# Low words of the second weight tile on GpSimd by halves, and the last output tile finished by column halves

## The chip, the cores and the metric

The kernel runs on one core of one Trainium2 chip. Its engines are TensorE (PE, with its weight loads shown apart as PEld), VectorE (DVE), ScalarE (ACT), GpSimd (POOL) and SyncE (SP, which here only issues DMAs). The metric is the device time of one execution in microseconds; less is better.

## What is computed

Retention (attention with a decay per head, no softmax) over 8 batches, 8 heads, 576 positions of 64, followed by a feed-forward layer:

```python
scores = scale * np.matmul(q, k.transpose(0, 1, 3, 2))
ret = scores * Dmat                      # Dmat = gamma[h] ** (i - j) for i >= j, else 0
x = np.matmul(ret, v)                    # laid out as 4608 tokens x 512
h = x @ w_in                             # 512 x 2048
g = h - np.tanh(h)
out = g @ w_out                          # 2048 x 512, fp32
```

Products of the feed-forward layer are made in three passes: every fp32 operand is split into a high word (rounded to the matmul's format) and a low word (the rest), and high x high, high x low and low x high are added up in PSUM.

## The kernel before

The 576 positions are cut into nine chunks of 64; a chunk of all 8 batches is a block of 512 tokens (n = 0 to 8). The weights are 16 tiles of w_in and 16 of w_out, each 128 x 512, which arrive as 64-bit words and are turned into a high and a low word on the chip.

**The conversion of a weight tile** runs over three engines. ACT makes a mask from the raw words in two steps (a Tanh, L130 or L157, and an Abs, L135, in `guard` and `guard_end`); DVE puts the 32-bit value together in three integer steps (`h_shift` L140, `l_shift` L143, `h_top` L146); ACT casts the value to the high word (L198 and L200 in `unit`, L165 in `second`); and the low word is the value minus the high word, one subtraction (`finish`, L213), on DVE except for the first tile, which has it on GpSimd.

**The start.** Chunk 0 of the retention runs first, for the eight batches in turn. Then `second` converts w_in tile 1 by column halves, and in between it starts tile 2, whose mask is called `ahead`: the Tanh before the halves, the Abs after the cast of the first half. The low word of tile 1 is left in the list `last`; the next call of `finish`, which comes behind the `h_shift` of tile 2, makes it on DVE in one piece. The loop over `seq` then runs `mm1(n, f)`, twelve matmuls that give the hidden tile h of block n and weight tile f: for f = 1, eight matmuls with high words (x high, x low), then four with low words of the weights (columns of the first half, then of the second). The high half of tile 2 is what `mm1(0, 2)` begins with. In the code the order of each engine's instructions is the order in which they are written, and each waits for those whose results it reads.

**The end.** `stage_b(8, ...)` runs `mm2(8, f)`, the second product of block 8: for each f twelve matmuls into four PSUM tiles o_0 to o_3 (128 tokens x 512 each). The last two f (14 and 15) run together, in groups of three matmuls, ordered by `groups`: (s, t) is f = 14 + s and output tile t. When a tile has its last product, `store_last` copies it to SBUF (o_1 on DVE, the others on ACT) and issues two DMAs of 64 rows x 2 KB to the output: the first from SP, the second from ACT (for o_0 both from SP). There is nothing behind the last of them but the end of the program.

The trace writes names without block and tile numbers: `wi<-mi` is a cast of a w_in tile, `o<-wo,gh` a second product with the high word gh, `gl` and `gs` the low word and a buffer that holds both.

Of the kernel before, what the change touches and what calls it, by code (L numbers as in the profile page):

```python
# [9 lines left out]
F32 = mybir.dt.float32  # L10
# [4 lines left out]
ALU = mybir.AluOpType  # L15
# [3 lines left out]
NT, DM, DF = B * S, H * D, 2048  # L19
P = 128  # L20
NF = DF // P
NCC = DM // P
C = 64
NC = S // C
BLK = B * C
# [73 lines left out]
def retention_ffn(ctx: ExitStack, tc: tile.TileContext, ins, out, spill, wvar):  # L99
    nc = tc.nc  # L100
# [4 lines left out]
    psp = ctx.enter_context(tc.tile_pool(name="psp", bufs=1, space=PSUM))  # L105
# [6 lines left out]
    win, wout, wraw, masks = {}, {}, {}, {}  # L112
# [21 lines left out]
    def guard_end(m):  # L134
        nc.scalar.activation(m.bitcast(F32), m, AF.Abs, scale=HI_BITS)  # L135

    halves = (slice(0, DM // 2), slice(DM // 2, DM))
# [10 lines left out]
    def second(low):  # L148

        t, f = stream[1]  # L150
        hw, lw, z = wraw[t, f][:, :, 1], wraw[t, f][:, :, 0], masks.pop((t, f))
        del wraw[t, f]

        w = const.tile([P, 2, 2, DM // 2], F32R, tag="wi14", name="wi1")
        win[f] = w
        ahead = masks[stream[2]] = pool.tile([P, DM], I32, tag="cv", bufs=4, name="ahead")
        nc.scalar.activation(ahead, wraw[stream[2]][:, :, 1].bitcast(F32), AF.Tanh, scale=STEP)  # L157
        ops = (h_shift, l_shift, h_top)
        for place_, (n, op) in enumerate(((0, 0), (0, 1), (1, 0), (0, 2), (1, 1), (1, 2))):
            at = halves[n]  # L160
            ops[op](z[:, at], hw[:, at], lw[:, at])
            if place_ == 0:
                low()
            if op == 2:
                nc.scalar.copy(w[:, n, 0], z[:, at].bitcast(F32))  # L165
                if n == 0:
                    guard_end(ahead)
        at_["guard"] = 3
        last.append(("i", w, z))

    def unit(k):

# [46 lines left out]
    last, going, pace = [], [], []  # L219
# [285 lines left out]
    gs, ops, homes, obs = {}, {}, {}, {}  # L505
# [55 lines left out]
    def mm2(n, f, at=-1, between=None):  # L561
        first, final = (turn[0], turn[-1]) if n == 1 else (0, NF - 1)
        if f == first:
            ops[n] = [psp.tile([P, DM], F32, tag=f"o{t}", bufs=1, name=f"o{n}_{t}") for t in range(4)]
        if f != final:
            order = [(f, t, k) for k in range(3) for t in range(4)]
        elif n < NC - 1:
            order = [(f, t, k) for t in range(4) for k in range(3)]
        else:

            groups = [(0, 0), (0, 1), (1, 0), (1, 1), (0, 2), (1, 2), (0, 3), (1, 3)]
            order = [(f - 1 + s, t, k) for s, t in groups for k in range(3)]
        for place_, (f_, t, k) in enumerate(order):
            if place_ == at:
                between()
            g, a = [(gs[n, f_][0], 0), (gs[n, f_][0], 1), (gs[n, f_][1], 0)][k]
            nc.tensor.matmul(  # L577
                ops[n][t], g[:, t * P : (t + 1) * P], wout[f_][:, a, :],
                start=(f_ == first and k == 0), stop=(f_ == final and k == 2),
            )  # L580
            if (k, t) == (1, 2):
                middle = tc.nc.cur_bb.bb.instructions[-1].name
            if f_ == final and k == 2:
                (store_last if n == NC - 1 else store)(n, t)
        return middle

    def store(n, t):
# [150 lines left out]
    for j in range(B - 1):  # L738
# [8 lines left out]
        o = psp.tile([P, 8, C], F32, tag=("o2", "o3", "own")[j % 3], bufs=1, name=f"own_first{j}")[:, :4]  # L747
# [26 lines left out]
    next(final_item)  # L774
    lows.pop(0)()
    second(lows.pop())
    assert not lows
    at_["convert"] = 2
# [30 lines left out]
    first = 2 * B  # L809
# [100 lines left out]
    for k, (n, f) in enumerate(late):  # L910
        if k in (3, 16, 29):
            follow, scale = entry3(first + (0, 2, 5)[(3, 16, 29).index(k)], rest)
        if 0 < k < len(late) - 1:
            words(*late[k + 1])
        if k < len(late) - 2:
            resume(*late[k + 2])
        for ahead in (4, 5) if k == 0 else (5,):
            if k + ahead < len(late):
                fetch(*late[k + ahead])
        if k in (3, 16, 29):  # L920

            follow()
        if k in (6, 19):
            scale()
        if k in (7, 20):
            load_part(rest[0], 0)
        if k in (10, 23):
            prep(rest.pop(), 0)
        for _ in range(2 if k < 4 else 1):
            step()  # L930
        for _ in range((k > 5) + (19 < k < 26)):
            next(summed)
        if k < len(late) - 1:
            mm2(n, f)
        for _ in range({0: 3, 1: 3, 2: 3, 3: 2}.get(k, 4 < k < 16 or 21 < k < 24)):
            raw_words(*raws.pop(0))
# [258 lines left out]
    def stage_b(n, m0):  # L1195

        fetch(n, 3)
        for f in range(NF):
# [20 lines left out]
            if (n, f) != (NC - 1, NF - 2):  # L1219
                middle = mm2(n, f, later or -1, turn_)  # L1220
# [10 lines left out]
    for f in range(NF):  # L1231
        mm1(2, f)
        if f == 0:
            mm2(*late[-1])
        if f == 1:
            scale()
        for _ in range(2):
            next(summed, None)
        if f == 2:
            load_turn(2, 0)  # L1240
        if f == 6:
            prep_turn(2, 0)
            load_turn(1, 0)
            load_turn(1, 1)
        if f in (9, 10):
            prep_turn(1, f - 9)
        if 10 < f < 14:
            fetch(2, f - 11)
        if f > 13:
            split(2, f - 14, fetched.pop((2, f - 14)), False)  # L1250
# [75 lines left out]
```

## Time and profile before

| | us |
|---|---|
| median of 3 runs | 848.39 |
| the runs | 847.99 to 848.69 |
| the profiled execution, whole | 849.77 |
| its span, first to last instruction | 848.0 |
| TensorE busy in the span | 840.1 (99%) |
| VectorE, ScalarE, GpSimd busy | 483.4, 362.6, 82.5 |

The profiled execution lasted 1.77 us longer than its span, and 1.38 us longer than the median of the runs. Times in the rows below are microseconds from the start of the span. A matmul's row covers its way through the array and so overlaps the next; the step from start to start is what one costs in a stream. DVE, ACT and POOL rows overlap their neighbours by some 0.05 to 0.1 us for the same reason.

### The profile page before, as it was taken

The page shows a single profiled execution, that of the slowest core. Times are in us where ns is not written, and L with a number is a line of the kernel's source. Part 1 is how long each engine was busy: PE and PEld are TensorE (multiplying, and loading weights), DVE is VectorE, ACT ScalarE, POOL GpSimd, SP SyncE. Part 2 cuts the span into 40 slices and gives each one's busy share as a digit, 9 for nine tenths or more (in the row PEclk, how much of TensorE's full clock was granted, in tenths as well). Part 3 has the DMA queues.
Part 4 walks back from the last instruction along what each step waited for, and adds up shares of the span by engine and source line. Part 5 has one row for each costly group of instructions (what it writes and reads, how often), then busy time and mean ns, then how long its engine had stood idle before and what let it go on. Part 6 is the DMA issues. An engine that isn't in the chain of part 4 may idle for free.

```text
span 848.0 us, 18635 instructions
## 1 busy us (share of the span) xinstructions
PE 840.1 (99%) x7694; PEld 694.0 (82%) x7694; DVE 483.4 (57%) x824; ACT 362.6 (43%) x732; POOL 82.5 (10%) x68
## 2 busy tenths in 40 slices
PE   8999999999999999999999999999999999999998
PEld 7788888888888888888888888888888888888886
DVE  5989878787567675344346755434456554443321
ACT  5887765454335454223244543322245532232321
POOL 0110002020000002111110001212100021121100
PEclk9999999999999999999999999999999999999999
DMA  9977978884787788444477665534677364452542
GB/s 342 321 293 225 371 232 300 243 280 132 224 272 271 228 308 249 149 153 170 132 236 224 209 181 194 187 125 170 207 214 209 108 201 171 133 191 75 147 115 62
DMA packets 71380, 174.95 MB, mean 206 GB/s; under 512 B 8704, under 2 KB 10368, under 8 KB 66048
## 3 DMA queue, kind: packets, MB, share of 16 engines
q1 hardware_dynamic: 70768, 172.85, 62.1%
q8 instruction: 60, 0.98, 0.5%
q10 hardware_dynamic: 528, 0.92, 0.3%
q14 instruction: 24, 0.20, 0.1%
HBM read 124.72 MB, written 48.76 MB: 205 GB/s over the span
## 4 chain that ended last, share of the span: by engine, by line
PE 97%; DVE 1%; ACT 1%; DMA 1%; issue 0%
PE o L577 32%; PE o L1136 15%; PE h L520 15%; PE pnew L1105 7%; PE pv L1105 7%; PE pown L1105 4%; PE py L1105 4%; PE pz L1105 4%; PE s L357 3%; PE new L357 2%; PE own L357 2%; DMA a<-in_first_dram 1%; PE wps L628 1%; ACT th L1155 0%; PE s_first L357 0%; PE new_first L357 0%
## 5 line engine op out<-in xcount | busy, mean ns | idle before, releaser
L577 PE MATMUL o<-wo,gh 128*128 128x512 f32 x608 | 156.0, 393 | 0.0
L577 PEld LDWEIGHTS o<-wo,gh 128*128 128x128 f32 x608 | 112.6, 188 | 24.6 <-DVE ob L599 0.4
L1159 POOL TENSOR_TENSOR c<-c,th 128x512 f32<-128x512 f32 x48 | 62.0, 1295 | 517.8 <-ACT th L1155 399.5
L1155 ACT ACTIVATE th<-c 128x512 f32<-128x512 f32 x72 | 45.5, 632 | 148.6 <-DVE c L1169 97.4
L520 PE MATMUL h<-xh,wi 128*128 128x512 f32 x384 | 98.1, 392 | 0.8 <-ACT wi L198 0.6
L520 PEld LDWEIGHTS h<-xh,wi 128*128 128x128 f32 x384 | 71.3, 188 | 17.0 <-ACT wi L198 1.1
L577 PE MATMUL o<-wo,gl 128*128 128x512 f32 x304 | 84.2, 389 | 0.0
L1136 PE MATMUL o<-wo,gs 128*128 128x512 f32 x288 | 70.6, 389 | 0.0
L577 PEld LDWEIGHTS o<-wo,gl 128*128 128x128 f32 x304 | 57.1, 188 | 11.9
L1136 PEld LDWEIGHTS o<-wo,gs 128*128 128x128 f32 x288 | 54.1, 188 | 11.2
L1105 PE MATMUL pnew<-xhv,ws 128*128 128x512 f32 x192 | 59.5, 391 | 0.3
L577 PE MATMUL o<-wo,gs 128*128 128x512 f32 x240 | 59.5, 394 | 0.0
L1105 PE MATMUL pv<-xhv,ws 128*128 128x512 f32 x192 | 59.1, 389 | 0.0
L357 PE MATMUL own<-qk,state 64*64 64x64 f32 x896 | 55.2, 221 | 0.0
L1165 DVE TENSOR_TENSOR work<-pown,work 128x512 f32<-128x512 f32 x24 | 16.6, 690 | 66.6 <-PE pown L1105 66.6
L357 PE MATMUL own<-qk,vr 64*64 64x64 f32 x928 | 54.0, 218 | 0.4 <-issue 0.4
L577 PEld LDWEIGHTS o<-wo,gs 128*128 128x128 f32 x240 | 44.4, 188 | 9.5
L520 PE MATMUL h<-xl,wi 128*128 128x512 f32 x192 | 52.1, 390 | 0.0
L1136 PE MATMUL o<-wo,gh 128*128 128x512 f32 x192 | 48.9, 389 | 0.0
L357 PEld LDWEIGHTS own<-qk,vr 64*64 64x64 f32 x928 | 45.1, 135 | 0.5 <-issue 0.5
L357 PEld LDWEIGHTS own<-qk,state 64*64 64x64 f32 x896 | 44.7, 135 | 0.0
L1121 DVE TENSOR_TENSOR gl<-s,gh 128x512 fp32r<-128x512 f32 x44 | 30.0, 688 | 23.5 <-PE o L577 13.2
(162 smaller groups left out, 1520.7 us busy)
## 6 DMA issues: line engine op xcount, KB each, us to landing
ws<-wvar_dram SPq DMA_DIRECT2D x41, 1024.0 KB, 4.9
s<-spill_dram SPq DMA_DIRECT2D x94, 256.0 KB, 4.2
qk<-in_qkv_dram SPq DMA_DIRECT2D x29, 512.0 KB, 4.8
vr<-in_qkv_dram SPq DMA_DIRECT2D x29, 512.0 KB, 4.9
spill_dram<-c SPq DMA_DIRECT2D x48, 256.0 KB, 2.6
spill_dram<-g SPq DMA_DIRECT2D x36, 256.0 KB, 3.5
rwi<-in_w_in_dram SPq DMA_DIRECT2D x16, 512.0 KB, 6.5
rwo<-in_w_out_dram SPq DMA_DIRECT2D x16, 512.0 KB, 5.4
```

What stands on the lines that cost most here:

```text
L357: nc.tensor.matmul(out_, w, x, start=start, stop=stop)
L520: nc.tensor.matmul(hp, win[f][:, cc // 2, a, cc % 2 * P : (cc % 2 + 1) * P], x[:, cc, :], start=(k == 0), stop=(k == 3 * NCC - 1))
L577: nc.tensor.matmul(ops[n][t], g[:, t * P : (t + 1) * P], wout[f_][:, a, :], start=(f_ == first and k == 0), stop=(f_ == final and k == 2),)
L628: nc.tensor.matmul(wps[:, :cols], warm[:, :P], warm[:, :cols], start=True, stop=True)
L1105: nc.tensor.matmul(into, w[:, a, k], x[:, k], start=start and i == 0, stop=i == len(terms) - 1, skip_group_check=not start,)
L1121: nc.vector.tensor_tensor(gl, g, gh.bitcast(F32), op=ALU.subtract)
L1136: nc.tensor.matmul(ops[n][t], g[:, t * P : (t + 1) * P], wout[f][:, a, :], start=(j == 0 and f == fs[0] and k == 0), stop=last_,)
L1155: nc.scalar.activation(th, c, AF.Tanh)
L1159: nc.gpsimd.tensor_tensor(c, c, tanh(c), op=ALU.subtract)
L1165: nc.vector.tensor_tensor(u2, y, u2, op=ALU.add)
```

## The change

Two edits, far apart in the program.

At the start, in `second`: the Abs of tile 2's mask comes right behind its Tanh, before the halves of tile 1 and so before both casts of tile 1 on ACT. The low word of tile 1 is made on GpSimd, one subtraction for each half right behind that half's cast; tile 1 is no longer put in `last`, so that `finish` finds nothing to do behind the `h_shift` of tile 2.

At the end, in `mm2` for the last block: the three products (0, 3) of the last output tile with f = 14 move ahead of (0, 2) and close that tile's sum over f = 0 to 14, which DVE copies to SBUF. The products (1, 3) with f = 15 leave the groups and come last, as six matmuls of 256 columns, three for each column half, each half in a PSUM bank of its own (tag `h`). DVE adds each half to the copy, and a DMA of 128 rows x 1 KB stores it: the first half from SP, the second from ACT.

```diff
         nc.scalar.activation(ahead, wraw[stream[2]][:, :, 1].bitcast(F32), AF.Tanh, scale=STEP)
+        guard_end(ahead)
         ops = (h_shift, l_shift, h_top)
...
             if op == 2:
                 nc.scalar.copy(w[:, n, 0], z[:, at].bitcast(F32))
-                if n == 0:
-                    guard_end(ahead)
+                nc.gpsimd.tensor_tensor(w[:, n, 1], z[:, at].bitcast(F32), w[:, n, 0].bitcast(F32), op=ALU.subtract)
         at_["guard"] = 3
-        last.append(("i", w, z))
...
-            groups = [(0, 0), (0, 1), (1, 0), (1, 1), (0, 2), (1, 2), (0, 3), (1, 3)]
+            groups = [(0, 0), (0, 1), (1, 0), (1, 1), (0, 3), (0, 2), (1, 2)]
...
-                start=(f_ == first and k == 0), stop=(f_ == final and k == 2),
+                start=(f_ == first and k == 0), stop=(f_ == (final - 1 if n == NC - 1 and t == 3 else final) and k == 2),
...
+            if f == final and n == NC - 1 and t == 3 and k == 2:
+                nc.vector.tensor_copy(obs[n][:, t], ops[n][t])
+        if f == final and n == NC - 1:
+            ob = obs[n][:, 3]
+            for queue, cols in zip((nc.sync, nc.scalar), halves):
+                o = psp.tile([P, BLK], F32, tag="h", bufs=2, name=f"o{n}_3_{cols.stop}")[:, : DM // 2]
+                for k, (part, a) in enumerate(((0, 0), (0, 1), (1, 0))):
+                    nc.tensor.matmul(o, gs[n, f][part][:, 3 * P :], wout[f][:, a, cols], start=(k == 0), stop=(k == 2))
+                nc.vector.tensor_tensor(ob[:, cols], o, ob[:, cols], op=ALU.add)
+                queue.dma_start(out[6:8, n * C : (n + 1) * C, cols], ob[:, cols])
```

VectorE at the start, before, from the last step of tile 1 on (mi_324 and wi_346 are tile 1, ahead and wi_383 tile 2, mi_362 tile 3):

```order
L146 SCALAR_TENSOR_TENSOR mi_324<-rwi_181,mi_324 128x256
L140 SCALAR_TENSOR_TENSOR ahead<-rwi_183,ahead 128x512
L213 TENSOR_TENSOR wi_346<-mi_324,wi_346 128x2x256
L143 SCALAR_TENSOR_TENSOR ahead<-rwi_183,ahead 128x512
L146 SCALAR_TENSOR_TENSOR ahead<-rwi_183,ahead 128x256 x2
L140 SCALAR_TENSOR_TENSOR mi_362<-rwi_253,mi_362 128x512
```

And in the changed kernel (its line numbers and buffer numbers are shifted by one; tile 2 is wi_384, tile 3 mi_363):

```order
L146 SCALAR_TENSOR_TENSOR mi_324<-rwi_181,mi_324 128x256
L140 SCALAR_TENSOR_TENSOR ahead<-rwi_183,ahead 128x512
L143 SCALAR_TENSOR_TENSOR ahead<-rwi_183,ahead 128x512
L146 SCALAR_TENSOR_TENSOR ahead<-rwi_183,ahead 128x256 x2
L140 SCALAR_TENSOR_TENSOR mi_363<-rwi_253,mi_363 128x512
```

The 512-column subtraction (L213) between the first and the second step of tile 2 is gone from VectorE; on GpSimd two of 256 columns (L167 of the changed kernel) stand behind the low word of tile 0.

ScalarE at the same place, before:

```order
L157 ACTIVATE ahead<-rwi_183 128x512
L165 CAST wi_346<-mi_324 128x256
L135 ACTIVATE ahead<-ahead 128x512
L165 CAST wi_346<-mi_324 128x256
L130 ACTIVATE mi_362<-rwi_253 128x512
```

And changed:

```order
L157 ACTIVATE ahead<-rwi_183 128x512
L135 ACTIVATE ahead<-ahead 128x512
L166 CAST wi_346<-mi_324 128x256 x2
L130 ACTIVATE mi_363<-rwi_253 128x512
L135 ACTIVATE mi_363<-mi_363 128x512
```

The Abs (L135) of tile 2 no longer waits behind the first cast of tile 1.

TensorE at the end of the program, before (wo_1101 is f = 14, wo_1201 is f = 15; gs holds both words for f = 14):

```order
L577 MATMUL o_1_8671<-wo_1201,gh_15_8896 128x512 x2
L577 MATMUL o_1_8671<-wo_1201,gl_15_8897 128x512
L577 MATMUL o_2_8672<-wo_1101,gs 128x512 x3
L577 MATMUL o_2_8672<-wo_1201,gh_15_8896 128x512 x2
L577 MATMUL o_2_8672<-wo_1201,gl_15_8897 128x512
L577 MATMUL o_3_8673<-wo_1101,gs 128x512 x3
L577 MATMUL o_3_8673<-wo_1201,gh_15_8896 128x512 x2
L577 MATMUL o_3_8673<-wo_1201,gl_15_8897 128x512
```

And changed:

```order
L576 MATMUL o_1_8672<-wo_1202,gh_15_8897 128x512 x2
L576 MATMUL o_1_8672<-wo_1202,gl_15_8898 128x512
L576 MATMUL o_3_8674<-wo_1102,gs 128x512 x3
L576 MATMUL o_2_8673<-wo_1102,gs 128x512 x3
L576 MATMUL o_2_8673<-wo_1202,gh_15_8897 128x512 x2
L576 MATMUL o_2_8673<-wo_1202,gl_15_8898 128x512
L591 MATMUL o_3_256_8945<-wo_1202,gh_15_8897 128x256 x2
L591 MATMUL o_3_256_8945<-wo_1202,gl_15_8898 128x256
L591 MATMUL o_3_512_8951<-wo_1202,gh_15_8897 128x256 x2
L591 MATMUL o_3_512_8951<-wo_1202,gl_15_8898 128x256
```

Three matmuls of o_3 now stand ahead of the six of o_2, and three of 512 columns became six of 256. On VectorE a copy of o_3 and two adds of 256 columns follow the copy of o_1; ScalarE has one copy less.

## Rows read from the trace of the kernel before

**Rows 1.** The page of the profile, its head and part 1: busy time of each engine, share of the span, instructions.

```profile
span 848.0 us, 18635 instructions
...
PE 840.1 (99%) x7694; PEld 694.0 (82%) x7694; DVE 483.4 (57%) x824; ACT 362.6 (43%) x732; POOL 82.5 (10%) x68
```

**Rows 2.** The waits of TensorE over the whole span: engine, line, whom it waited for, us in total, times, longest.

```profile
PE h L520 <- ACT wi L198: 0.6, 1, 0.6
PE own L357 <- issue: 0.4, 1, 0.4
```

**Rows 3.** The chain of work that ended last, from 19.4 to 23.1 us: start, us, what.

```profile
19.37 0.54 ACT ahead L135
...
19.93 0.69 DVE ahead L140
20.63 0.60 DVE wi L213
21.23 0.61 DVE ahead L143
...
22.21 0.43 DVE ahead L146
...
22.66 0.41 ACT wi L198
...
23.11 0.98 PE h L520 x3
```

**Rows 4.** The timeline of the same stretch, ScalarE, VectorE and TensorE: start, us, engine, line, operation; in brackets the idle time before it and its releaser.

```profile
17.74 0.66 ACT L157 ACTIVATE ahead<-rwi 128x512 int32<-128x512 f32 x1
18.96 0.41 ACT L165 CAST wi<-mi 128x256 fp32r<-128x256 f32 x1 [0.56 <-DVE mi L146]
19.29 0.43 DVE L146 SCALAR_TENSOR_TENSOR mi<-rwi,mi 128x256 int32<-128x256 int32 x1
19.81 0.39 ACT L165 CAST wi<-mi 128x256 fp32r<-128x256 f32 x1
21.39 1.09 PE L520 MATMUL h<-xh,wi 128*128 128x512 f32 x4
```

**Rows 5.** The timeline of GpSimd, at six places of the first 145 us.

```profile
13.84 1.27 POOL L213 TENSOR_TENSOR wi<-mi,wi 128x512 fp32r<-128x512 f32 x1 [13.40 <-ACT wi L200]
31.09 0.62 POOL L787 TENSOR_TENSOR krows<-krows,vtab 128x256 f32<-128x256 f32 x1 [15.98 <-DVE mi L146]
...
59.12 1.04 POOL L295 TENSOR_TENSOR vr<-vr,vtab 128x512 f32<-128x512 f32 x1 [1.67 <-DMA vr<-in_qkv_dram]
...
137.34 1.25 POOL L295 TENSOR_TENSOR vr<-vr,vtab 128x512 f32<-128x512 f32 x1 [58.32 <-DMA vr<-in_qkv_dram]
138.63 0.98 POOL L295 TENSOR_TENSOR one<-one,vtab 128x256 f32<-128x256 f32 x1
139.57 1.18 POOL L295 TENSOR_TENSOR one<-one,qtab 128x256 f32<-128x256 f32 x1
```

**Rows 6.** The timeline of VectorE beside those of GpSimd (60.74 stands for an undisturbed one of the same shape).

```profile
59.13 1.57 DVE L140 SCALAR_TENSOR_TENSOR mi<-rwi,mi 128x512 int32<-128x512 int32 x1
60.74 0.69 DVE L143 SCALAR_TENSOR_TENSOR mi<-rwi,mi 128x512 int32<-128x512 int32 x1
...
137.61 1.53 DVE L551 TENSOR_TENSOR s<-s,th 128x512 f32<-128x512 f32 x1
139.06 1.10 DVE L881 TENSOR_TENSOR vt<-wi 128x512 f32<-128x512 f32 x1
140.08 1.22 DVE L558 TENSOR_TENSOR gl<-s,gh 128x512 fp32r<-128x512 f32 x1
```

**Rows 7.** The timeline of the end: the copies of o_1 and of the last two tiles, and ScalarE's DMA issues behind them (ACTq is ScalarE's issuing of DMAs).

```profile
841.13 0.69 DVE L613 COPY ob<-o 128x512 f32<-128x512 f32 x1 [4.69 <-PE o L577]
...
842.49 0.59 ACT L615 COPY ob<-o 128x512 f32<-128x512 f32 x1 [1.45 <-PE o L577]
843.10 0.50 ACTq L618 DMA_DIRECT2D out_dram<-ob  x1
843.85 0.58 ACT L615 COPY ob<-o 128x512 f32<-128x512 f32 x1 [0.77 <-PE o L577]
844.46 0.50 ACTq L618 DMA_DIRECT2D out_dram<-ob  x1
```

**Rows 8.** The DMA view of two stretches, issues with KB each and us from issue to landing: the store of o_2 (843.3 to 844.2 us), then the store of o_3 (844.2 to 848 us, two rows).

```profile
out_dram<-ob ACTq DMA_DIRECT2D x1, 128.0 KB, 2.9
...
out_dram<-ob SPq DMA_DIRECT2D x1, 128.0 KB, 2.3
out_dram<-ob ACTq DMA_DIRECT2D x1, 128.0 KB, 2.6
```

**Rows 9.** The landings of the table qtab (128 rows of 1 KB, read), over the whole span.

```profile
DMA to landing us min/median/max: 2.6/4.1/5.5
```

**Rows 10.** The chain again, 24 matmuls of 512 columns in a stream, from 744 us.

```profile
744.14 5.44 PE o L1136 x24
```

**Rows 11.** Groups of instructions by shape: a weight load of the second product, and a VectorE subtraction with 256 columns (count, busy us, mean ns, idle before).

```profile
L577 PEld LDWEIGHTS o<-wo,gh 128*128 128x128 f32 x608 | 112.6, 188 | 24.6 <-DVE ob L599 0.4 <-ACT gh L1120 0.3
...
L386 DVE TENSOR_TENSOR xl<-own_first,xh 128x256 fp32r<-128x256 f32 x4 | 1.5, 417 | 0.0
```

## The prediction

> **What bounds the kernel now.** First the page: TensorE is busy 840.1 of 848.0 us [rows 1], so time can be won only where it stands still, or before its first and behind its last matmul. Then its waits: in the whole span one is long enough to matter and released by another engine, 0.62 us for ScalarE's cast of weight tile 2, and one of 0.4 us has no releaser [rows 2]. The reader is to see in the chain of waits what stands ahead of that cast: from 19.93 to 22.63 us nothing but VectorE steps of tile 2, and among them the low word of tile 1 (L213, 0.60 us) [rows 3]. VectorE is the late engine there; ScalarE and TensorE wait for it. TensorE's real loss is a little more than 0.62: its last four matmuls of h_1 begin at 21.39 [rows 4], a matmul in a stream takes 5.44 / 24 = 0.227 us [rows 10], so the next could begin at 21.39 + 4 x 0.227 = 22.30; it begins at 23.11 [rows 3], 0.81 later. From 23.11 on TensorE runs without a pause but for the 0.4, so whatever tile 2 gains or loses reaches the end unless that pause takes it up.
>
> The end of the program is the timeline behind the last matmul: ScalarE copies o_3 from 843.85 for 0.58 us, both queues issue its stores at 844.46 [rows 7], the later lands 2.6 us on [rows 8], at 847.06, and 0.94 us on the span ends.
>
> **Part 1, the start: what leaves VectorE's chain.** The low word (0.60) goes. The Abs of tile 2 comes sooner: its Tanh ends at 17.74 + 0.66 = 18.40, so it is done by some 19.05 and not at 19.9 [rows 3, 4], and `h_shift` of tile 2 no longer waits; it could start as soon as VectorE has issued the step before it, some 19.62, and not at 19.93. That is 0.31 + 0.60 = 0.91 us less on the chain. The casts of tile 1 on ScalarE shift from 18.96 to 19.0 and from 19.81 to 19.75, which costs nothing.
>
> **What comes in.** GpSimd gets two subtractions of 256 columns with both inputs in SBUF. The nearest row is the 128x256 product at 31.09, 0.62 us [rows 5]. Both run in the middle of VectorE's stream, and VectorE's three integer steps also read two SBUF operands each. What the trace shows of such pairs decides this part. At 59.12 GpSimd starts a product of 1.04 us; VectorE's `h_shift` of 59.13 then takes 1.57 us where its kind takes 0.69, and ends 0.54 us behind GpSimd's end. From 137.34 to 141.3 both have work queued and take turns, three times over: each VectorE step ends 0.55 us behind GpSimd's, and GpSimd's 128x256 products take 0.98 and 1.18 us, their 0.62 and the wait for VectorE's step [rows 5, 6]. So beside each other they do not share; each holds the other up for its whole length.
>
> Now the sum in these terms. VectorE's last step of tile 1 ends at 19.29 + 0.43 = 19.72 [rows 4]. GpSimd is ready from about 19.45 (the first cast is done), takes its turn at 19.72 and ends at 20.34. `h_shift` of tile 2 ends 0.55 later, at 20.89. By then the second cast is long done (20.15), GpSimd takes its second turn and ends at 21.51, `l_shift` ends at 22.06. Before it ended at 21.23 + 0.61 = 21.84 [rows 3]. What follows is unchanged, so tile 2 is late by 0.22 us. If VectorE wins the first boundary, `h_shift` runs first and GpSimd comes in at the two gaps behind it; two turns of 0.62 are then in the chain all the same, some 0.1 us of them beside VectorE's own gaps, and the loss is about 0.1. I take **+0.2 us**. Ends: -0.8 if the two do not block each other at all (worked out below), +0.4 if each turn costs 0.1 more.
>
> The Trainium skill has a rule that speaks against this edit (SBUF — State Buffer, Who interferes with whom): a VectorE instruction with two SBUF inputs and a GpSimd one that reads SBUF use one port pair, which whichever issues first keeps to the end of its instruction. By that rule, with which the rows agree, the sum is the +0.2 again; without it, it would be the -0.8.
>
> TensorE's own need is covered: `mm1(0, 1)` wants the low words of the first half at 21.39 and of the second at 21.39 + 2 x 0.227 = 21.84; they are there at 20.34 and 21.51. Were the second late, its cover is the pause of 0.8 us that follows. Nothing else waits on GpSimd: its next work is at 31.09.
>
> **Part 2, the end: TensorE and VectorE.** The last tile's six 128x256 matmuls carry the columns of three. At 2.4 GHz 512 columns take 0.213 of the 0.227 us, so 0.013 us an instruction lies beside the columns; half the columns are 0.107 + 0.013 = 0.120, six are 0.72 for 0.68: +0.04. The other end is that a weight load's 188 ns [rows 11] becomes the step, since a short matmul no longer hides it: 6 x 0.188 - 0.68 = +0.45. I take +0.04, because in the stream of 0.227 the load costs nothing visible.
>
> The Trainium skill gives a weight load as its columns over 1.2 (TensorE: Matmul & The Clock Gate, LDWEIGHTS), 107 ns for 128; by that estimate it stays hidden behind a half, as I take it, and no row here shows a 256-column stream with fp32 weights.
>
> The copy of o_3 on VectorE follows that of o_1 (841.13, 0.69 [rows 7]) and ends by 842.5, under TensorE's products of o_2: no cost. The last add has 256 columns, 0.42 us [rows 11], and takes the place of the 0.58 copy: -0.16. The last issue moves from 844.46 to 844.46 + 0.04 - 0.16 = 844.34.
>
> **Part 2, the stores.** The three matmuls of (0, 3) now stand ahead of o_2, which is done 3 x 0.227 = 0.68 us later; its two stores are issued at 843.78 and not at 843.10, just ahead of the last two on the same two queues (each issue takes 0.5 us, so the last fit behind at about 844.3). What was spread over 1.36 us comes in 0.56. Before, the store of o_2, issued while earlier ones were still under way, took up to 2.9 us to land, and that of o_3, with the queues nearly empty, 2.3 and 2.6 [rows 8]. The last landing is thus 844.34 + 2.6 = 846.94 to 844.34 + 2.9 = 847.24, against 847.06: -0.12 to +0.18, middle +0.03. Rows of 1 KB for 2 KB are not shown for a write to the output; the nearest, qtab's 128 rows of 1 KB read, land in 2.6 at best [rows 9], 0.3 over the fastest of these stores, so up to +0.3 more. I take **0.0 us** for the whole end; bounds -0.15 and +0.18 + 0.3 + 0.45 = +0.9.
>
> **The sum** against the profiled execution: 848.0 + 0.2 + 0.0 = 848.2 of span; on the median, 848.39 + 0.2 = **848.6 us**.
>
> **Rivals.**
> 1. The two engines do not hold each other up at the start (GpSimd slips into VectorE's gaps). Tile 2 is then 0.91 early, TensorE goes on at 22.30 behind its own matmuls and wins the 0.8; with -0.1 at the end 847.5. For it: the low word of tile 0 already runs on GpSimd in 1.27 us, no longer than others of its size [rows 5]. Against it: the four stretched VectorE rows [rows 6]. It decides itself in whether VectorE's steps between 19.6 and 22 us stay at 0.69.
> 2. The end loses: the weight load sets the step of the short matmuls, and the four stores in a row land late. With the start's +0.2 that is up to 848.39 + 0.2 + 0.9 = 849.5, half of it 849.0. It decides from a step of over 0.15 us between the last six matmuls, or a landing over 2.8.
> 3. The start does nothing: the 0.4 us pause of TensorE without a releaser [rows 2] ends at a time of its own and swallows the 0.2: 848.4. Nothing speaks for an absolute time but that no engine released it.
>
> **How the numbers follow.** Forecast 0.60, rival 1 0.15, rival 2 0.15, rival 3 0.08, none of these 0.02. The forecast's own spread is 848.3 to 848.9, with the runs of before 0.35 us to either side of their median. The range takes in the three rivals: 847.4 to 849.3; rival 2 at its worst is left out. 0.2% of the time is 1.7 us, about what a measurement of this kernel can tell from no change; no case here leaves it, so the chances are 0.02 faster, 0.95 within, 0.03 slower, the last two hundredths from an end that adds up all its bounds and a delay that I have not seen.
>
> **What would show it.** Right: two GpSimd rows of 0.6 to 1.2 us between 19.4 and 21.6 us, VectorE's `h_shift` and `l_shift` of tile 2 at about 1.2 us each instead of 0.69, and TensorE's wait for the cast of tile 2 at 0.8, not gone; at the end a last issue near 844.3 + 0.2 and a landing of 2.6 to 2.9. Wrong: VectorE rows of 0.69 there and TensorE without a wait before h_2; or the last six matmuls at 0.19 apart; or a pause of TensorE later on that was not there.

## The result and the profile after

| | us |
|---|---|
| before, median (6 runs, beside the changed kernel) | 848.23 (847.99 to 849.50) |
| the changed kernel, median (6 runs) | 854.41 (854.06 to 854.85) |
| ratio | 1.0072, 95% interval 1.0061 to 1.0083 |
| the profiled execution, whole, and its span | 854.25 and 852.5 |

The change costs 6.2 us. The page of the changed kernel, against [rows 1]: the span is 4.5 us longer, and TensorE is busy for 1.3 us less. (The traced execution of before was 1.38 us slower than its median, so the spans differ by less than the medians.)

```profile
span 852.5 us, 18646 instructions
...
PE 838.8 (98%) x7697; PEld 693.5 (81%) x7697; DVE 486.0 (57%) x826; ACT 362.3 (43%) x731; POOL 84.9 (10%) x70
```

So TensorE has no more to do than before. The timeline of the end shows that the time isn't lost ahead of the last issue either, which stands at 842.95 and stood at 844.46 before [rows 7] (start, us, engine, line, operation; L591 are the short matmuls, L592 the additions, L593 the new stores, L627 the other ones):

```profile
841.59 0.40 PE L591 MATMUL o<-wo,gh 128*128 128x256 f32 x2
...
842.14 0.78 DVE L592 TENSOR_TENSOR ob<-o,ob 128x256 f32<-128x256 f32 x2 [1.02 <-PE o L591]
842.18 0.28 PE L591 MATMUL o<-wo,gl 128*128 128x256 f32 x1
842.40 0.50 ACTq L627 DMA_DIRECT2D out_dram<-ob  x1
842.95 1.43 ACTq L593 DMA_DIRECT2D out_dram<-ob  x1
842.96 0.62 SPq L593 DMA_DIRECT2D out_dram<-ob  x1
```

The six short matmuls start at 841.59 to 842.18, one every 0.12 us; the stores are issued at 842.95. The program's last wait is SP's for these stores (waits of SP: us in total, times, longest); in the same view of before it is 1.9 in total and 1.0 at the longest.

```profile
SPq L1331 <- DMA out_dram<-ob: 7.7, 2, 6.3
```

What the DMA engines do meanwhile is in the table of windows of 1 us (window, us, busy time of the five engines with counts, granted clock of TensorE, mean busy share of the 16 DMA engines, GB/s):

```profile
842.00:843.00 1.00, 0.46 (x4) 0.25 (x3) 0.78 (x2) 0.37 (x1) 0.00 (x0) 1.00 0.93 215
...
844.00:845.00 1.00, 0.00 (x0) 0.00 (x0) 0.00 (x0) 0.00 (x0) 0.00 (x0) 1.00 0.58 171
845.00:846.00 1.00, 0.00 (x0) 0.00 (x0) 0.00 (x0) 0.00 (x0) 0.00 (x0) 1.00 0.12 31
846.00:847.00 1.00, 0.00 (x0) 0.00 (x0) 0.00 (x0) 0.00 (x0) 0.00 (x0) 1.00 0.14 47
...
849.00:850.00 1.00, 0.00 (x0) 0.00 (x0) 0.00 (x0) 0.00 (x0) 0.00 (x0) 0.50 0.13 47
850.00:851.00 1.00, 0.00 (x0) 0.00 (x0) 0.00 (x0) 0.00 (x0) 0.00 (x0) 0.50 0.12 43
851.00:852.00 1.00, 0.00 (x0) 0.00 (x0) 0.00 (x0) 0.00 (x0) 0.00 (x0) 0.50 0.01 5
```

The reader is to see the share: from 845 to 851 it is 0.12 to 0.14, and 2 / 16 is 0.125. That is what two DMA engines of sixteen give that are busy all the time: they carry the last 256 KB, at some 47 GB/s, and fourteen stand still. 256 packets of 1 KB at 48 a microsecond are 5.3 us. In the DMA view of the microsecond from 848 the two queues (q1 is SP's, q10 ScalarE's; packets, MB, share) have half of that each, so they share the same two engines:

```profile
q1 hardware_dynamic: 24, 0.02, 6.9%
q10 hardware_dynamic: 24, 0.02, 6.9%
```

A count of packets says two as well. The DMA view of the end (838 to 853 us), before and after:

```profile
DMA packets 640, 1.05 MB, mean 70 GB/s; under 512 B 128, under 2 KB 128, under 8 KB 640
...
DMA packets 740, 1.05 MB, mean 70 GB/s; under 512 B 100, under 2 KB 356, under 8 KB 740
```

Before, eight stores of 64 rows are 512 packets of data and 128 short ones, 16 for each store. After, six such stores leave 96 short ones, so the two new stores have 4, two each, as if every engine that takes part in a store ended with one. In e3, e4 and e5 below the same view counts 160, 98 and 130: again 16 for each store over 64 rows and 2 for each over 2 x 64.

At the start things went as forecast. The timeline there, against [rows 3, 4] (L167 are GpSimd's subtractions, L140 and L143 the first two integer steps of tile 2, L519 the matmuls of h_0 and h_2):

```profile
15.62 2.09 PE L519 MATMUL h<-xh,wi 128*128 128x512 f32 x8 [0.21 <-DVE xh L735]
...
18.66 2.02 POOL L167 TENSOR_TENSOR wi<-mi,wi 128x256 fp32r<-128x256 f32 x2 [3.50 <-ACT wi L166]
...
18.84 1.23 DVE L140 SCALAR_TENSOR_TENSOR ahead<-rwi,ahead 128x512 int32<-128x512 int32 x1
20.11 1.12 DVE L143 SCALAR_TENSOR_TENSOR ahead<-rwi,ahead 128x512 int32<-128x512 int32 x1
...
22.51 0.74 PE L519 MATMUL h<-xh,wi 128*128 128x512 f32 x2 [0.84 <-ACT wi L197]
```

VectorE's steps take 1.23 and 1.12 us, where this form takes 0.69 undisturbed [rows 6], TensorE waits 0.84 for tile 2, and from the first matmul of h_0 to that of h_2 it is 22.51 - 15.62 = 6.89 us. Before, the timeline has h_0 at 16.43 and h_2 at 23.11, 6.68 apart.

**A measure for the runs.** h_0 begins at 15.5 to 16.4 us, depending on the execution, so two stretches are compared below: the *start*, from h_0's first matmul to h_2's, and the *tail*, from the first matmul behind the last product of o_1 to the end of the span. Products over the same columns lie in it in both orders of the end: twelve of 512 columns before, nine of 512 and six of 256 after. It begins, in the timelines of before and after, with

```profile
840.93 0.84 PE L577 MATMUL o<-wo,gs 128*128 128x512 f32 x3
...
839.54 1.52 PE L576 MATMUL o<-wo,gs 128*128 128x512 f32 x6
```

With the spans to two decimals (from a window over the whole span), the tail is 847.98 - 840.93 = 7.05 before and 852.46 - 839.54 = 12.92 after. The start is 6.68 before and 6.89 after. So the change is +0.21 at the start and +5.87 in the tail. The traces with the old end unchanged (before, and e1, e6, e7 and e8 below) have tails of 7.05 to 7.07, so a tenth of a microsecond can be read in it.

What lies between, the *middle*, is the same work in every kernel, and it takes 816.9 to 817.8 us (818.95 in e6) from one traced execution to the next (817.82 before, 817.03 after). So differences of some tenths there are not read as effects. It holds TensorE's 0.4 us pause of before [rows 2] (0.2 in e7, none in the others), 0.4 us for a cast of weights in e9, and 1.2 us for a VectorE step in e6; whether the work added in e6 brought that one is open.

### The profile page after: what moved, and what is told of

The parts are those of the page before. It is cut to its first block, busy times and chain, and to the rows that moved or that the text cites. A ratio compares the mean times of both kernels' runs of the same rounds, so it can differ in the third digit from the quotient of the medians.

```text
span 852.5 us, 18646 instructions
## 1 busy us (share of the span) xinstructions
PE 838.8 (98%) x7697; PEld 693.5 (81%) x7697; DVE 486.0 (57%) x826; ACT 362.3 (43%) x731; POOL 84.9 (10%) x70
## 4 chain that ended last, share of the span: by engine, by line
PE 96%; DVE 1%; ACT 1%; DMA 1%; issue 0%; SPq 0%
PE o L576 31%; PE o L1145 15%; PE h L519 15%; PE pnew L1114 7%; PE pv L1114 7%; PE pown L1114 4%; PE py L1114 4%; PE pz L1114 4%; PE s L356 3%; PE new L356 2%; PE own L356 2%; DMA rwi<-in_w_in_dram 1%; ACT th L1164 0%; DVE c L1182 0%; DVE th L1186 0%
## 5 line engine op out<-in xcount | busy, mean ns | idle before, releaser
L519 PE MATMUL h<-xh,wi 128*128 128x512 f32 x384 | 97.9, 392 | 1.1 <-ACT wi L197 0.8
L519 PEld LDWEIGHTS h<-xh,wi 128*128 128x128 f32 x384 | 71.4, 188 | 16.9 <-ACT wi L197 1.3
L519 PE MATMUL h<-xl,wi 128*128 128x512 f32 x192 | 52.1, 390 | 0.0
L1130 DVE TENSOR_TENSOR gl<-s,gh 128x512 fp32r<-128x512 f32 x44 | 30.0, 689 | 23.1 <-PE o L576 11.8
```

The source lines that it names most:

```text
L519: nc.tensor.matmul(hp, win[f][:, cc // 2, a, cc % 2 * P : (cc % 2 + 1) * P], x[:, cc, :], start=(k == 0), stop=(k == 3 * NCC - 1))
L1130: nc.vector.tensor_tensor(gl, g, gh.bitcast(F32), op=ALU.subtract)
```

## The experiments

Theory A: a DMA whose access pattern has an outermost dimension of 2 is carried by two DMA engines, the same two for both queues. Rival B: rows of 1 KB are slow. Rival C: four stores in a row are slow. For the start: GpSimd and VectorE hold each other up, against no such block.

| run | median us (range, runs) | before beside it | ratio (95%) | start | middle over 800 | tail |
|---|---|---|---|---|---|---|
| e1_head | 848.81 (848.25 to 849.86, 11) | 848.35 | 1.0007 (0.9999 to 1.0016) | 6.89 | 17.43 | 7.06 |
| e2_tail | 854.29 (853.97 to 855.27, 4) | 848.35 | 1.0072 (1.0059 to 1.0086) | 6.67 | 17.16 | 13.04 |
| e3_tail64 | 849.03 (848.57 to 850.95, 11) | 848.35 | 1.0011 (1.0002 to 1.0020) | 6.68 | 17.58 | 7.52 |
| e4_one_store | 853.37 (853.21 to 853.71, 4) | 848.35 | 1.0061 (1.0046 to 1.0076) | 6.70 | 17.02 | 12.20 |
| e5_first_half | 851.43 (851.15 to 852.55, 4) | 848.51 | 1.0037 (1.0023 to 1.0051) | 6.69 | 17.14 | 10.19 |
| e6_pool_beside | 849.52 (848.90 to 851.72, 10) | 848.51 | 1.0015 (1.0006 to 1.0024) | 7.48 | 18.95 | 7.06 |
| e7_memset_beside | 848.63 (848.07 to 849.59, 10) | 848.51 | 1.0001 (0.9992 to 1.0010) | 7.12 | 17.76 | 7.07 |
| e8_guard_sooner | 847.98 (847.76 to 848.48, 11) | 848.51 | 0.9993 (0.9985 to 1.0002) | 6.38 | 17.28 | 7.05 |
| e9_guard_and_split | 848.64 (847.95 to 849.29, 11) | 848.51 | 0.9998 (0.9989 to 1.0007) | 6.37 | 17.65 | 7.30 |
| e10_guard_and_banks | 848.40 (848.10 to 849.53, 11) | 848.51 | 1.0000 (0.9991 to 1.0008) | 6.39 | 17.06 | 7.32 |
| e11_mended_change | 848.75 (848.63 to 849.23, 11) | 848.51 | 1.0001 (0.9992 to 1.0010) | 6.87 | 16.98 | 7.36 |
| e12_third_queue | 848.85 (848.62 to 849.70, 11) | 848.43 | 1.0003 (0.9994 to 1.0012) | 6.37 | 16.94 | 7.93 |

What a run's start and tail gain or lose against before adds up to the difference of its medians within 0.3 us; in e7 it is 0.34, for a reason given there.

### Which edit: e1 and e2

e1 is the kernel before with the first edit alone:

```diff
+        guard_end(ahead)
...
-                if n == 0:
-                    guard_end(ahead)
+                nc.gpsimd.tensor_tensor(w[:, n, 1], z[:, at].bitcast(F32), w[:, n, 0].bitcast(F32), op=ALU.subtract)
...
-        last.append(("i", w, z))
```

> The start's edit alone. Theory (GpSimd and VectorE hold each other up, and the whole loss of the changed kernel comes from its end): within 0.5 us of the kernel before, from h_0's first matmul to h_2's first 6.9 us as in the changed kernel, not 6.68 as before. Rival (the start is to blame through something later that the profile hides): slower by several us.

e2 is the second edit alone:

```diff
-            groups = [(0, 0), (0, 1), (1, 0), (1, 1), (0, 2), (1, 2), (0, 3), (1, 3)]
+            groups = [(0, 0), (0, 1), (1, 0), (1, 1), (0, 3), (0, 2), (1, 2)]
...
+                queue.dma_start(out[6:8, n * C : (n + 1) * C, cols], ob[:, cols])
```

> The end's edit alone. Theory: the whole loss is here, +5.5 to +6.5 us against the kernel before; behind the last TensorE record 10.4 us pass instead of 4.2. Rival: about 0.

Measured: e2 has all of the loss, 5.9 us of median, in its tail (+5.99); its start is as before. e1 has the start's +0.21 and a tail as before. The two edits don't touch each other.

### The stores: e3, e4 and e5

e3 is e2, with each column half stored by two DMAs of 64 rows of 1 KB:

```diff
-                queue.dma_start(out[6:8, n * C : (n + 1) * C, cols], ob[:, cols])
+                for u, q in enumerate((nc.sync, nc.scalar)):
+                    q.dma_start(out[6 + u, n * C : (n + 1) * C, cols], ob[half(u), cols])
```

> The end's edit alone, but each column half stored by two DMAs of 64 rows x 1 KB (one from SP, one from ACT) in place of one DMA over 2 x 64 rows. Theory A (a store whose outermost dimension is 2 is carried by two DMA engines): the loss is gone, -0.3 to +0.5 us against the kernel before, data done about 1 to 2 us after the last issue on all 16 engines. Theory B (rows of 1 KB are slow to write): still +4 us or more. Theory C (four stores close together are slow): still +4 us or more.

e4 is the kernel before, with only its last tile's two stores joined into one over 2 x 64 rows of 2 KB:

```diff
+        if t == 3:
+            nc.sync.dma_start(out[6:8, n * C : (n + 1) * C], ob)
+            return
         for u in range(2):
```

> The kernel before with one thing changed: the last tile is stored by one DMA over 2 x 64 rows of 2 KB from SP, where there were two of 64 rows. Theory A (outermost dimension 2, two engines of some 24 GB/s each): 256 KB take about 5.3 us instead of 1.0, so +4 to +5 us. Theories B and C (rows of 1 KB, or four stores in a row): about 0, since rows stay 2 KB and nothing comes closer together.

e5 is e2, with the first column half stored by one DMA over 2 x 64 rows and the second by two of 64 rows:

```diff
-                queue.dma_start(out[6:8, n * C : (n + 1) * C, cols], ob[:, cols])
+                if cols.start == 0:
+                    queue.dma_start(out[6:8, n * C : (n + 1) * C, cols], ob[:, cols])
+                    continue
+                for u, q in enumerate((nc.sync, nc.scalar)):
+                    q.dma_start(out[6 + u, n * C : (n + 1) * C, cols], ob[half(u), cols])
```

> The end of the changed kernel; of its two column halves the first is stored by one DMA over two parts of 64 rows, as there, the second by two DMAs of 64 rows of 1 KB. If the two slow DMAs of the changed kernel went one after the other through the same two DMA engines, one of them by itself is done in half the time: 256 packets at about 48 a microsecond, which the trace of the changed kernel shows, are 5.3 us, less for what is under way before the rest is done, so the end comes 2 to 3.5 us later than before, about 851. If each is slow by itself whatever the other does, the time stays at about 854.3. If only the second queue's DMA is slow, it is at about 849.

e3 settles B and C: the same rows of 1 KB, in more DMAs and just as close together, cost 0.47 us of tail (7.52 for 7.05) and not 5.9; its median is 0.7 us over before, a little more than was expected. e4 settles it from the other side: rows of 2 KB, one DMA in place of two, nothing else changed, and the loss is there (+5.15 in the tail). Its windows of 1 us:

```profile
847.00:848.00 1.00, 0.00 (x0) 0.00 (x0) 0.00 (x0) 0.00 (x0) 0.00 (x0) 0.50 0.13 51
848.00:849.00 1.00, 0.00 (x0) 0.00 (x0) 0.00 (x0) 0.00 (x0) 0.00 (x0) 0.50 0.13 51
849.00:850.00 1.00, 0.00 (x0) 0.00 (x0) 0.00 (x0) 0.00 (x0) 0.00 (x0) 0.50 0.13 51
```

The same two engines' share, 51 GB/s with 2-KB rows for 47 with 1-KB ones: the row's length hardly matters. e5 halves the bytes on the slow path, and the loss is halved: its tail is 10.19, and with both halves stored by 64 rows it is 7.32 (e10 below), so 2.87 us; 128 KB at 48 GB/s are 2.7. In its windows the slow share stands alone after 847, when the other half's stores are through:

```profile
846.00:847.00 1.00, 0.00 (x0) 0.00 (x0) 0.00 (x0) 0.00 (x0) 0.00 (x0) 0.50 0.47 125
847.00:848.00 1.00, 0.00 (x0) 0.00 (x0) 0.00 (x0) 0.00 (x0) 0.00 (x0) 0.50 0.14 48
848.00:849.00 1.00, 0.00 (x0) 0.00 (x0) 0.00 (x0) 0.00 (x0) 0.00 (x0) 0.50 0.04 14
```

So in the changed kernel the two slow stores stand in each other's way, though they come from two queues. Theory A holds; B and C fall as causes of the loss.

The Trainium skill states this rule (DMA: Bandwidth & Descriptors, Why a DMA increments its semaphore by 16 and not by 1): the number of engines is the largest, up to 16, that divides the slowest dimension (of a size over 1) of both access patterns, and for DMAs issued from SP or ScalarE those with the lowest numbers are taken. By it 2 x 64 rows go to two engines, the same for every such DMA, and 64 rows to sixteen; the shares and packet counts above and e5 agree on both. Which two they are, no trace here shows, and no size but 64 and 2 was tried.

### The start: e6, e7 and e8

e6 is the kernel before, with GpSimd's two subtractions added; they write a tile that nobody reads:

```diff
+        scratch = const.tile([P, 2, DM // 2], F32, name="scratch")
...
                 nc.scalar.copy(w[:, n, 0], z[:, at].bitcast(F32))
+                nc.gpsimd.tensor_tensor(scratch[:, n], z[:, at].bitcast(F32), w[:, n, 0].bitcast(F32), op=ALU.subtract)
```

> The kernel before with the two GpSimd subtractions added, with the same inputs, into a tile that nobody reads; VectorE still makes the low words that are used. If GpSimd and VectorE hold each other up whenever both work, VectorE's low word and its two steps behind it each end later by some 0.5 to 0.6 us, and the third group's first matmul stands 7.2 to 8.0 us behind the first group's (6.68 before): 848.9 to 849.6 in all. If they work side by side without loss, it is 6.68 and 848.4.

e7 has a fill of such a tile in their place, at the same point (`behind` makes the fill wait for the cast):

```diff
+        scratch = const.tile([P, 2, DM // 2], F32, name="scratch")
...
                 nc.scalar.copy(w[:, n, 0], z[:, at].bitcast(F32))
+                cast = last_on(tc, nc.scalar.engine)
+                nc.gpsimd.memset(scratch, float(n))
+                behind(tc, cast)
```

> The kernel before with two GpSimd fills of a tile of 128x512 that nobody reads, each behind one of tile 1's casts: GpSimd works beside VectorE's steps, but reads nothing from SBUF. If what holds VectorE up is GpSimd's reading of two operands (or its arithmetic), VectorE's steps there keep their 0.68 us and the third group stands 6.68 us behind the first as before: 848.4. If any work of GpSimd's does it, VectorE's steps are stretched to 0.9 to 1.2 us as with the subtractions, and the third group comes 7.2 to 7.8 us behind the first.

e8 is the kernel before with the guard sooner, the low word left on VectorE:

```diff
+        guard_end(ahead)
         ops = (h_shift, l_shift, h_top)
...
-                if n == 0:
-                    guard_end(ahead)
```

> The kernel before with the other half of the start's edit alone: the guard on tile 2's words ahead of tile 1's, the low words still on VectorE. If the two guarded steps set the third group, it comes about 0.3 us sooner (6.37 us behind the first group, 6.68 before), 848.05. If tile 1's low words, now behind the guard's steps, are what TensorE waits for instead, the second group starts later by up to 0.4 us and the time is 848.3 to 848.7.

In e6, VectorE's timeline is stretched as in the changed kernel, on work that doesn't use GpSimd's result:

```profile
18.62 2.03 POOL L167 TENSOR_TENSOR scratch<-mi,wi 128x256 f32<-128x256 f32 x2 [3.53 <-ACT wi L166]
19.10 0.94 DVE L140 SCALAR_TENSOR_TENSOR ahead<-rwi,ahead 128x512 int32<-128x512 int32 x1 [0.21 <-ACT ahead L135]
19.97 1.23 DVE L215 TENSOR_TENSOR wi<-mi,wi 128x512 fp32r<-128x512 f32 x1
21.12 0.68 DVE L143 SCALAR_TENSOR_TENSOR ahead<-rwi,ahead 128x512 int32<-128x512 int32 x1
```

The first two of VectorE's steps run beside GpSimd's work (18.62 to 20.65) and take 0.94 and 1.23; the third, behind it, 0.68. The start is 0.8 longer. In e7 GpSimd works beside the same steps and they aren't stretched (VectorE's steps, GpSimd's second fill and ScalarE's Tanh, timeline):

```profile
19.80 0.69 DVE L140 SCALAR_TENSOR_TENSOR ahead<-rwi,ahead 128x512 int32<-128x512 int32 x1 [0.65 <-ACT ahead L135]
20.41 0.68 DVE L217 TENSOR_TENSOR wi<-mi,wi 128x512 fp32r<-128x512 f32 x1
...
20.18 0.53 POOL L168 MEMSET scratch<- 128x512 f32 x1 [0.36 <-ACT wi L166]
...
18.27 0.67 ACT L157 ACTIVATE ahead<-rwi 128x512 int32<-128x512 f32 x1 [1.01 <-DMA rwi<-in_w_in_dram]
```

The fill from 20.18 to 20.71 lies across both steps, and they keep 0.69 and 0.68. e7's start of 7.12 is not the fill's doing: in the profiled execution ScalarE's Tanh of tile 2 stood 1.01 us for the arriving weights. So it isn't GpSimd's being at work as such that blocks, nor its writing. The Trainium skill makes the same cut (SBUF — State Buffer, Who interferes with whom): a VectorE instruction with two SBUF inputs meets a GpSimd one that reads SBUF, not one that only writes it. e6 and e7 agree; but a subtraction differs from a fill by its arithmetic too, and no run here parts the two.

e8 takes 0.30 off the start and nothing off the tail; TensorE's wait for tile 2 is 0.36, for 0.6 before [rows 2] (timeline):

```profile
22.03 0.74 PE L519 MATMUL h<-xh,wi 128*128 128x512 f32 x2 [0.36 <-ACT wi L197]
```

This splits the first edit: the guard alone gives 6.68 - 6.38 = 0.30, and the low words on GpSimd cost 6.89 - 6.38 = 0.51 (e1 against e8).

### Looking for a version better than both: e9 to e12

e9 is e8, with o_3's copy by halves on two engines:

```diff
+        elif t == 3:
+            nc.vector.tensor_copy(ob[:, halves[0]], o[:, halves[0]])
+            nc.scalar.copy(ob[:, halves[1]], o[:, halves[1]])
```

> The guard sooner as in the run beside it, and the last output tile's copy by column halves on VectorE and ScalarE at once in place of one copy of 512 columns, its stores by 64 rows as before. If the end is set by the last copy, the halves give 0.16 to 0.3 us on top of the guard's: 847.8. If the copies' start on two engines costs what the halves save, it is the same as the run beside it.

e10 is e8 with the second edit, its stores by 64 rows of 2 KB behind the second addition:

```diff
-                queue.dma_start(out[6:8, n * C : (n + 1) * C, cols], ob[:, cols])
+                if cols.start > 0:
+                    for u, q in enumerate((nc.sync, nc.scalar)):
+                        q.dma_start(out[6 + u, n * C : (n + 1) * C], ob[half(u)])
```

> The guard sooner with the low words on VectorE, and the end with the last tile's last products by column halves in banks of their own as in the changed kernel, but stored behind the second addition by two DMAs of 64 rows of 2 KB, as before. If the stores' outer dimension was all that was wrong with the end, the last issue comes some 0.3 us sooner than before, and the time is 0.3 us (guard) and 0.2 to 0.3 us (end) below before: 847.7 to 847.9. If the banks' six matmuls or two additions cost something that the slow stores hid, it is 848.0 or more.

e11 is the changed kernel with that same edit of the stores.

> The whole change, only the last tile's two stores by 64 rows of 2 KB behind the second addition. If the time lost in the changed kernel is the stores' alone, 848.2 to 848.6: 0.2 to 0.5 us lost at the start by GpSimd's subtractions, 0.2 to 0.3 won at the end. If another 0.5 us or more is lost somewhere, 849.0 or more.

e12 is e10, with one store of the tile before on GpSimd's queue:

```diff
-            queue = nc.scalar if u == 1 and t > 0 else nc.sync
+            queue = nc.gpsimd if u == 1 and t == 2 else nc.scalar if u == 1 and t > 0 else nc.sync
```

> The guard sooner and the mended end, only that the third output tile's second store goes out from GpSimd's queue in place of ScalarE's, so that ScalarE's last issue has no other of its own 0.05 us before it. If that neighbour is why ScalarE's last issue took 0.83 us (0.50 with the guard alone), it takes 0.50 again, the last data land some 0.3 us sooner, and the time is 848.1 beside the guard's 848.0 and the mended end's 848.4. If two queues issuing at one moment hold each other up whatever went before, it stays at 0.8 and 848.4. If GpSimd's issue and landing are slow, its store is the last and the time is 849 or more.

In e9 the halves don't run at once. The timeline has ScalarE's copy behind VectorE's and released by it:

```profile
842.91 0.42 DVE L614 COPY ob<-o 128x256 f32<-128x256 f32 x1 [2.03 <-PE o L576]
843.37 0.37 ACT L615 COPY ob<-o 128x256 f32<-128x256 f32 x1 [1.23 <-DVE ob L614]
```

From the start of the last matmul (842.49) to the last issue (843.77) it is 1.28 us, in e8 842.85 - 841.81 = 1.04: 0.24 more, which is the tail's 0.25 over e8's. Here both halves lie in one PSUM bank and in one tile of SBUF; which of the two makes the order was not tried apart.

e10 and e11 show what the end's edit is worth with stores over 64 rows: it loses a little, with tails of 7.32 and 7.36 for 7.05. The medians, 848.40 and 848.75, don't tell them from before. The timeline of e8 (two rows) and that of e10 show where it goes:

```profile
839.31 0.84 PE L576 MATMUL o<-wo,gs 128*128 128x512 f32 x3
...
842.85 0.50 ACTq L617 DMA_DIRECT2D out_dram<-ob  x1
```

```profile
839.21 1.52 PE L576 MATMUL o<-wo,gs 128*128 128x512 f32 x6
...
842.07 0.50 ACTq L629 DMA_DIRECT2D out_dram<-ob  x1
842.62 0.83 ACTq L595 DMA_DIRECT2D out_dram<-ob  x1
842.63 0.54 SPq L595 DMA_DIRECT2D out_dram<-ob  x1
```

From the beginning of the tail to the last ScalarE issue it is 3.41 us in e10 and 3.54 in e8, so 0.13 is won. But that issue now stands 0.05 us behind another of ScalarE's own and takes 0.83 us; in e8, with 0.86 us between them, it takes 0.50. And its data land 3.0 us after its start, for 2.6 in e8 (DMA views from the last issues on, e8 and e10):

```profile
out_dram<-ob ACTq DMA_DIRECT2D x1, 128.0 KB, 2.6
...
out_dram<-ob ACTq DMA_DIRECT2D x1, 128.0 KB, 3.0
```

e12 takes that neighbour away, and the issue is back at 0.50:

```profile
842.23 0.70 POOL L629 DMA_DIRECT2D out_dram<-ob  x1 [54.88 <-ACT ob L626]
842.52 0.50 ACTq L595 DMA_DIRECT2D out_dram<-ob  x1
842.53 0.54 SPq L595 DMA_DIRECT2D out_dram<-ob  x1
```

But the stores land later, in its DMA view 3.3 us (GpSimd's) and 3.5 (ScalarE's) after their issue, and the tail is 0.6 longer than e10's. So the neighbour sets the length of the issue; that the longer issue is why e10's data land late is not shown, and stores that crowd each other remain a rival. The fastest kernel measured is e8: 847.98 against 848.51, 0.30 us of it seen in its trace, and its interval of 0.9985 to 1.0002 just holds 1.

## Why the prediction was wrong

**The step that failed** is "Part 2, the stores": "The last landing is thus 844.34 + 2.6 = 846.94 to 844.34 + 2.9 = 847.24", with "up to +0.3 more" for 1-KB rows. The landings of 2.6 to 2.9 are those of DMAs with 64 rows outermost, and qtab's of one with 128. The new stores join two heads of the output, with 2 outermost, and no row of before shows such a pattern. I took the length of a row for what was new in them; e3 and e4 show that it hardly counts, and that the outermost dimension does: issued at 842.95, they move data until after 851, more than 8 us. That is +5.87 in the tail, outside of every bound. The diff had the pattern, and the rule of the Trainium skill named above (DMA: Bandwidth & Descriptors, Why a DMA increments its semaphore by 16 and not by 1) has two engines for it; a wait, a size and a burst were weighed there, the shape was not.

**Part 1, the start**, was right in its mechanism and its size: +0.2 forecast, +0.21 in the trace, VectorE's two steps at 1.23 and 1.12 ("about 1.2 us each"), TensorE's wait at 0.84 ("0.8"). The turns came as laid out: h_0 stands 0.81 us sooner after than before, so the forecast ends of 20.89 and 22.06 are 20.08 and 21.25 there, and the steps end at 20.07 and 21.23. Rival 1 (no mutual block) is refuted by e6. What the sum joined, e8 and e1 split: -0.30 and +0.51.

**Part 2, TensorE and VectorE**: a step of 0.12 for the short matmuls, as forecast; the weight load doesn't show. The last issue came sooner by the 0.12 of the sum, counted from the beginning of the tail: 3.53 before, 3.41 after (3.54 and 3.41 in e8 and e10). What the sum did not have is ScalarE's issue of 0.83 us right behind another and a landing of 3.0 over its 2.9: with stores over 64 rows the end costs 0.27 us (e10) where it had 0.0, inside of its bounds.

**Rival 2** ("the end loses") had the right sign, but not the mechanism of the loss: its price of at most +0.9 rested on the weight load's step, which didn't come, and on a landing over 2.8. The late landing came, 3.0 in e10, and is worth those 0.27 us, not the 5.87. **Rival 3**: the 0.4 us pause is missing from the changed kernel's profile, so nothing was there to swallow the start's loss; nor is it in the traces of most kernels with the old start.

## What to carry to other kernels

Before joining two DMAs into one, look at the outermost dimension of its access pattern: 2 x 64 rows were carried by two DMA engines at some 48 GB/s, where two DMAs of 64 rows used them all. At the end of a program all of that time counts; whether other work would cover it earlier on was not tried. An operation with two SBUF inputs that is moved to GpSimd beside such operations of VectorE's has not left VectorE's path: the low words took 0.69 us on VectorE, and on GpSimd they made the start 0.51 longer (e1 against e8). And stretches inside the program (from h_0 to h_2, from the last products of o_1 to the end) told apart tenths of a microsecond that the medians couldn't, where a stretch with the whole middle in it could not.

## What the hardware did that was not expected

- Two DMAs from two queues, each over 2 x 64 rows, share the same two DMA engines: one alone costs 2.9 us of tail (e5, 10.19 against 7.32 in e10), two cost 5.6 (12.92 against 7.36 in e11).
- Beside such a slow one, stores over 64 rows land late: in e5 the two of 64 KB issued with it and behind it landed 5.4 and 5.1 us after their issue, in e3 such stores took 2.5 and 2.3.
- A ScalarE issue of a DMA takes 0.50 us, but 0.83 when another of its own ended 0.05 us before (e5, e10 and e11, and 0.50 again in e12). The changed kernel's, over 2 x 64 rows at the same place, took 1.43, where SP's took 0.62.
- GpSimd's fill of 128x512 (0.53 us) runs beside VectorE's steps without any loss (e7); its subtraction of 128x256 holds them up by 0.25 to 0.55 us each (e6).
